# A fused attention and gated-MLP kernel: first batch pipelined by pairs of heads, first weights in fp32 behind it, last tokens of two batches moved into block 1

## Chip, cores, metric

The kernel runs on one core of one Trainium2 chip. The metric is the device time of one execution in microseconds (us). Each execution also records the mean clock that TensorE was granted, as a share of full speed.

Engine names: PE is TensorE (PEld its weight loads), DVE is VectorE, ACT is ScalarE, POOL is GpSimd, which issues the casting loads (fp32 read, fp16 written), SP is the engine that issues the first loads and the stores. A "strip" is one of the 12 groups of 128 hidden columns of the MLP; a "block" is 512 tokens of one batch that go through the MLP together. "Last tokens" are tokens 512 to 575 of a batch, which don't fill a group of 128; two batches share one.

## The reference, cut

```python
# q, k, v: (8 batches, 8 heads, 576 tokens, 64)
kv  = einsum('bhsd,bhse->bhde', k, v)
out = einsum('bhsd,bhde->bhse', q, kv)
x   = out / sqrt(mean(out * out, -1) + 1e-6) * g_norm      # then (4608, 512)
g, val  = x @ w_gate, x @ w_val                            # (512, 1536) each
ffn_out = (gelu(g) * val) @ w_out                          # (1536, 512)
y = x + sigmoid(x @ w_res) * ffn_out
```

## The kernel before

Where the traces were read for it, an engine ran its instructions in the order in which the program writes them. The attention of batch b is computed in small pieces that are put into "slots" between the MLP's strips of block b-1. Slots 0 to 11 of a block are its strips, the later ones its output rows. Block 0 is special: its output is accumulated strip by strip, so its slots run to 27.

The opening worked on batch 0 in halves of four heads, and the weights came by casting loads (fp32 in HBM, fp16 in SBUF) issued by GpSimd:

```python
for half in range(2):                      # fp32 loads on SP's queue, cast on the engines
    load_first("q", q, half)
    load_first("k", k, half)
    load_first_last(0, half)               # last tokens of k, v
    load_first_last(1, half)
    load_first("v", v, half)
# ... cast, transposes, kv, o, norm of one half, then of the other ...
nc.gpsimd.tensor_copy(out=hold, in_=s0["kv2"][0:1, 0, 0:1])   # waits for kv of half 0
load_wg(0)                                 # casting loads, 256 columns
load_wv(0)
# ... load_wg(i), load_wv(i), i = 1, 2, 3
```

The attention of batch 1, last tokens of batches 0 and 1 among it, all lay in block 0:

```python
plan = {                                   # NF = 12; attn_plan_1
    NF + 3: [attn_begin(1), a_qT(1, 0), a_qT(1, 1), load_batch(2), a_kv(1, 0, NP), a_rem_qT(1)],
    NF + 4: [a_rem_o(1), o[0]],            # a_rem_*: last tokens of two batches
    NF + 5: [o[1]], NF + 6: [o[2]], NF + 7: [o[3]],
    NF + 8: [a_norm(1), t[0], t[1], t[2], t[3], t[4]],
    2 * NF + 1: [x[0], x[1]],              # x: PE transposes of t, copied out by ACT
    2 * NF + 2: [x[2], x[3]],
    2 * NF + 3: [x[4]],                    # 27: behind the last step of block 0's output
}
# a_norm: 12 small DVE operations (a Newton iteration for 1/sqrt)
# plan_attn, batch 2 in block 1:
at(1, 2, by_token(2, "q"))                 # DVE: cast and reorder
at(1, 3, by_token(2, "k"), attn_begin(2), d_qT(2))
at(1, 4, a_kv(2, 0, 2))                    # PE: needs the cast k
# loads behind strip 2 of block 0, casting queue:
#   w_res, load_batch(1) = q, k, v, last tokens of k, v and of q (load_qr), then w_out in 3 pieces
```

## Time and profile before

| | before |
|---|---|
| median of 4 executions | 356.85 us (355.98 to 357.12) |
| span of the profiled execution | 354.6 us |
| busy share PE / DVE / ACT / POOL | 97% / 60% / 35% / 13% |
| third strip of block 0 starts | 23.35 us |
| first product with w_out | 47.07 us, after a wait of 0.60 |
| block 1's first product | 60.21 us |
| batch 2's kv product in block 1 | 69.14 us |
| first product of the last output row group | 347.60 us |

PE has work nearly all the time. The prediction below shows the page's lines.

### The profile page before, as it was taken

What the parts mean: (1) busy time and instruction counts of PE and PEld (TensorE: products, weight loads), DVE (VectorE), ACT (ScalarE), POOL (GpSimd) and SP (SyncE); (2) the same over time, 40 slices, a digit from 0 to 9 for tenths busy, and PEclk for the clock granted to TensorE, in tenths of its full rate; (3) what the DMA queues carried; (4) which work ended last, traced back from release to release, by engine and by line L of the source; (5) the groups of instructions that cost most, each with busy time, mean ns of one, the idle gap of its engine ahead of it and who ended that gap; (6) DMA issues with size and microseconds to landing.
All of it is one profiled execution on the core that took longest, in us unless ns stands there. A gap on an engine that the chain in (4) does not pass through costs nothing.

```text
span 354.6 us, 5021 instructions
## 1 busy us (share of the span) xinstructions
PE 343.0 (97%) x1905; PEld 168.9 (48%) x1905; DVE 214.1 (60%) x428; ACT 125.7 (35%) x215; POOL 47.7 (13%) x74
## 2 busy tenths in 40 slices
PE   6879999999999999999999999999999999999995
PEld 2554465454454445544554445444544444444443
DVE  5655448868757774676569656865587543343433
ACT  3653474253146222531363125422542233223320
POOL 1853330050050005000130023000000000000000
PEclk9999999999999999999999999999999999999999
DMA  8999999489699058904594369327000500020013
GB/s 250 221 180 201 193 203 142 137 137 106 160 164 131 2 133 167 153 0 118 136 166 36 86 169 175 24 61 194 0 2 30 133 31 0 30 87 5 1 31 89
DMA packets 77707, 37.95 MB, mean 107 GB/s; under 512 B 42226, under 2 KB 73202, under 8 KB 77682
## 3 DMA queue, kind: packets, MB, share of 16 engines
q0 software_dynamic: 39792, 17.70, 39.7%
q1 hardware_dynamic: 37728, 19.80, 20.6%
q8 instruction: 15, 0.25, 0.3%
q10 hardware_dynamic: 162, 0.13, 0.1%
q14 instruction: 10, 0.08, 0.1%
HBM read 38.80 MB, written 9.44 MB: 136 GB/s over the span
## 4 chain that ended last, share of the span: by engine, by line
PE 84%; DMA 9%; POOL 2%; DVE 1%; SPq 1%; ACT 0%; issue 0%; DVEq 0%
PE fps L348 25%; PE gps L315 23%; PE vps L315 23%; PE rps L335 8%; DMA wv<-in_moe_w_val_dram 4%; DMA wo<-in_moe_w_out_dram 4%; PE op L194 2%; PE kvp L165 2%; DMA vf<-in_v_dram 1%; POOL wg L120 1%; PE fps L377 1%; POOL wv L120 1%; PE orp L212 1%; PE kvp L172 0%; SPq L435 0%; DVE hid L304 0%
## 5 line engine op out<-in xcount | busy, mean ns | idle before, releaser
L315 PE MATMUL gps<-xT,wg 128*128 128x512 f16 (+2 forms) x448 | 112.3, 371 | 2.3 <-ACT xT L597 1.2
L304 DVE TENSOR_TENSOR hid<-ge,vps 128x512 f16<-128x512 f16 x108 | 73.5, 685 | 65.8 <-PE vps L315 59.3
L315 PE MATMUL vps<-xT,wv 128*128 128x512 f16 (+2 forms) x448 | 112.3, 371 | 0.0
L303 ACT ACTIVATE ge<-gps 128x512 f16<-128x512 f32 x108 | 64.4, 598 | 114.3 <-PE gps L315 105.2
L348 PE MATMUL fps<-wo,hid 128*128 128x512 f16 x420 | 96.9, 379 | 0.6 <-DMA wo<-in_moe_w_out_dram 0.6
L315 PEld LDWEIGHTS <-wv 128*128 128x128 f16 x448 | 43.4, 98 | 50.4 <-DMA wv<-in_moe_w_val_dram 0.3
L348 PEld LDWEIGHTS <-hid 128*128 128x128 f16 x420 | 40.8, 98 | 48.7 <-DMA wo<-in_moe_w_out_dram 0.8
L315 PEld LDWEIGHTS <-wg 128*128 128x128 f16 x448 | 42.0, 98 | 44.0 <-issue 2.7
L354 DVE SCALAR_TENSOR_TENSOR pf<-th,fps 128x512 f32<-128x512 f32 x35 | 23.8, 686 | 47.6 <-PE fps L348 47.6
L344 ACT ACTIVATE th<-rps 128x512 f32<-128x512 f32 x36 | 21.5, 598 | 79.5 <-PE rps L335 79.5
L335 PE MATMUL rps<-wr,xT 128*128 128x512 f16 x144 | 36.5, 379 | 0.0
L188 DVE TENSOR_REDUCE ss<-sq 128x8 f32<-128x512 f32 x32 | 21.5, 683 | 7.3 <-ACT sq L187 5.5
L359 DVE SCALAR_TENSOR_TENSOR osb<-pf,t 128x512 f32<-128x512 f32 x35 | 24.2, 691 | 1.1
L335 PEld LDWEIGHTS <-xT 128*128 128x128 f16 x144 | 14.1, 98 | 17.0
L187 ACT ACTIVATE sq<-op 128x512 f32<-128x512 f32 x28 | 16.7, 598 | 9.9 <-PE op L194 9.2
L727 POOL COPY hold<-qT 1x1 f16<-1x1 f16 x5 | 0.9, 177 | 138.2 <-DMA qT<-q 138.2
L252 DVE TENSOR_TENSOR t<-op,ny 128x512 f16<-128x512 f32 x28 | 17.8, 680 | 0.1
L271 DVE TENSOR_TENSOR t<-t,g 128x512 f16<-128x512 f16 x36 | 13.3, 417 | 0.0
L165 PE MATMUL kvp<-v,k 128*128 128x128 f16 x128 | 10.6, 219 | 2.4 <-DVE v L495 2.2
L165 PEld LDWEIGHTS <-k 128*128 128x128 f16 x128 | 8.9, 98 | 6.3 <-DVE v L495 1.9
L194 PEld LDWEIGHTS <-qT 128*128 128x128 f16 x112 | 8.4, 98 | 5.7
L194 PE MATMUL op<-kv,qT 128*128 128x128 f16 x112 | 10.8, 219 | 0.0
(96 smaller groups left out, 168.0 us busy)
## 6 DMA issues: line engine op xcount, KB each, us to landing
out_dram<-osb SPq DMA_DIRECT2D x32, 256.0 KB, 2.4
qraw<-in_q_dram POOLq DMA_DIRECT2D x7, 512.0 KB, 6.1
kraw<-in_k_dram POOLq DMA_DIRECT2D x7, 512.0 KB, 8.3
v<-in_v_dram POOLq DMA_DIRECT2D x7, 512.0 KB, 10.1
wo<-in_moe_w_out_dram POOLq DMA_DIRECT2D x3, 512.0 KB, 14.0
qf<-in_q_dram SPq DMA_DIRECT2D x2, 512.0 KB, 4.7
kf<-in_k_dram SPq DMA_DIRECT2D x2, 512.0 KB, 5.8
vf<-in_v_dram SPq DMA_DIRECT2D x2, 512.0 KB, 6.0
```

The source lines that it names most:

```text
L165: nc.tensor.matmul(ps, lhsT=k16[:, j, cs], rhs=v16[:, 2 * pr : 2 * pr + 2, j * D : (j + 1) * D], start=(j == 0), stop=False,)
L188: nc.vector.tensor_reduce(out=st[b]["ss"][:, j, :], in_=sq, op=ALU.add, axis=mybir.AxisListType.X)
L194: nc.tensor.matmul(ps[:, pr * P : (pr + 1) * P], lhsT=s["qT"][:, j, pr, :], rhs=s["kv2"][:, pr, :], start=True, stop=True)
L252: nc.vector.tensor_tensor(out=t_t[blk][:, jj, :].rearrange("p (h d) -> p h d", h=H), in0=s["o"][j].rearrange("p (h d) -> p h d", h=H), in1 ...
L303: nc.scalar.activation(out=ge, in_=gps, func=AF.Gelu)
L304: nc.vector.tensor_tensor(out=hids[blk][:, f, :], in0=ge, in1=vps, op=ALU.mult)
L315: nc.tensor.matmul(ps[:, j0 * P : j1 * P], lhsT=w[:, cc, :], rhs=xT_t[blk][:, j0:j1, cc, :], start=(cc == 0 and j0 == 0), stop=(cc == NP - ...
L335: nc.tensor.matmul(rps, lhsT=xT_t[blk][:, j, cc, :], rhs=wr16[:, cc, :], start=(cc == 0), stop=(cc == NP - 1),)
L344: nc.scalar.activation(out=th, in_=rps, func=AF.Tanh, scale=0.5)
L348: nc.tensor.matmul(fps, lhsT=hids[blk][:, f, j * P : (j + 1) * P], rhs=wo16[:, f, :], start=(f == 0), stop=(f == NF - 1))
L354: nc.vector.scalar_tensor_tensor(out=pf, in0=th, scalar=1.0, in1=fps, op0=ALU.add, op1=ALU.mult)
L359: nc.vector.scalar_tensor_tensor(out=osb, in0=pf, scalar=0.5, in1=t_t[blk][:, j, :], op0=ALU.mult, op1=ALU.add)
```

## The change

The intent: start on batch 0 sooner by loading and processing it in four pairs of heads; let the first weights follow on the same hardware queue, since SP is free to issue them early (in the kernel before its last load of the opening is issued by 7.22 us, and it issues no other before 40 us), and cast them on GpSimd and ACT; and take the last tokens of batches 0 and 1 out of block 0, with their loads behind w_out, so that w_out arrives sooner.

```diff
-for half in range(2): load_first("q", q, half) ... load_first("v", v, half)
+for i in range(2):
+    load_first_last(i, 0, nc.scalar)
+for pr in range(NP):                                   # 4 pairs
+    if pr == 2:
+        for i in range(2):
+            load_first_last(i, 1, nc.sync)
+    for which, t in (("q", q), ("k", k), ("v", v)):
+        load_first(which, t, pr)
+w_raw = {}                                             # first 256 columns, fp32
+for n, t in (("g", moe_w_gate), ("v", moe_w_val)):
+    ...
+    nc.sync.dma_start(out=w_raw[n], in_=t[:, 0 : WCS[0]].rearrange("(cc p) f -> p cc f", p=P))
...
+opening = """                                          # word: step, pair, [half], engine
+lc0P qc0A kc0A qT0 vc0D warm2 kv0 qc1P qo0D kvo0 warm1 kc1A o0 qT1 sq0 vc1D kv1 lc1P ...
+warm2 vc3D kv3 qo3A rd2 wcg0P kvo3 xT1 rt2 o3 xo1A ri2 t2 g0 wcg1P sq3a g1 wcv0P rd3a sq3b rd3b xT2 wcv1A
+w2 rt3 v0 xo2D gelu ri3 v1 t3a xT3a t3b v2 xo3aA xT3b xo3bD g2 w3 g3a v3a g3b v3b"""
...
 # attn_plan_1
-    NF + 3: [..., a_kv(1, 0, NP), a_rem_qT(1)],
-    NF + 4: [a_rem_o(1), o[0]], ...
-    NF + 8: [a_norm(1), t[0], t[1], t[2], t[3], t[4]],
+    NF + 3: [..., a_kv(1, 0, NP)],
+    NF + 4: [o[0], o[1]], ...
+    NF + 7: [a_norm(1, 0, NJ), t[0], t[1], t[2], t[3]],
     2 * NF + 1: [x[0], x[1]],
-    2 * NF + 2: [x[2], x[3]],
-    2 * NF + 3: [x[4]],
+    2 * NF + 3: [x[2], x[3]],
+at(1, 0, a_rem_qT(1))
+at(1, 1, a_rem_o(1))
+at(1, 2, a_norm(1, NJ, NJ + 1), t[NJ])                 # behind by_token(2, "q") in that slot
+at(1, 6, x[NJ])
+at(1, 7, a_x(1, NJ))
...
 for f in range(0, NF, 4):
     load_wo(f, f + 4)
+load_qr(0)                                             # no longer in the opening and load_batch(1)
+load_qr(1)
```

More of the change, by code (lines that the diff above doesn't have):

```diff
@@ L102, in load_batch @@
         load_last_kv(b)
-        load_qr(b)
+        if b > 1:
+            load_qr(b)
     def by_token(b, which):
@@ L222, in a_rem_o, with a_norm @@
         st[b]["o"][NJ] = o32
-    def a_norm(b):
+    def a_norm(b, j0, j1):
         s = st[b]
-        n = (NJ + (b % 2)) * H
-        ss = s["ss"].rearrange("p j h -> p (j h)")[:, 0:n]
+        if "rinv" not in s:
+            s["rinv"] = attnp.tile([P, NJ + 1, H], FP32, tag="ny", name="ny")
+        ss, yy = (t[:, j0:j1, :].rearrange("p j h -> p (j h)") for t in (s["ss"], s["rinv"]))
+        n = (j1 - j0) * H
         m = attnp.tile([P, (NJ + 1) * H], FP32, tag="nm", name="nm")[:, 0:n]
-        y = attnp.tile([P, (NJ + 1) * H], FP32, tag="ny", name="ny")
         a = attnp.tile([P, (NJ + 1) * H], FP32, tag="na", name="na")[:, 0:n]
         mh = attnp.tile([P, (NJ + 1) * H], FP32, tag="nh", name="nh")[:, 0:n]
-        yy = y[:, 0:n]
         nc.vector.tensor_scalar(out=m, in0=ss, scalar1=1.0 / D, scalar2=RMS_EPS, op0=ALU.mult, op1=ALU.add)
@@ L242, in a_norm @@
             nc.vector.scalar_tensor_tensor(out=yy, in0=a, scalar=1.5, in1=yy, op0=ALU.add, op1=ALU.mult)
-        s["rinv"] = y.rearrange("p (j h) -> p j h", h=H)
     def where(b, j):
@@ L425, with load_first, load_first_last @@
         raw[0, which] = t[:, 0 : H * NJ * D].rearrange("p (h x) -> p h x", h=H)
-    def load_first(which, t, half):
-        hs = slice(half * HH, (half + 1) * HH)
+    def load_first(which, t, pr):
+        hs = slice(2 * pr, 2 * pr + 2)
         nc.sync.dma_start(out=raw[0, which][:, hs, :], in_=rows4(t, 0, hs.start, hs.stop))
     last_raw = [consts.tile([R, H, D], FP32, name=f"{n}lf") for n in "kv"]
-    def load_first_last(i, half):
+    def load_first_last(i, half, queue):
         hs = slice(half * HH, (half + 1) * HH)
-        nc.sync.dma_start(
+        queue.dma_start(
             out=last_raw[i][:, hs, :], in_=(k, v)[i][0, hs, M0:S, :].rearrange("h s d -> s h d")
@@ L440 @@
     nc.scalar.dma_start(out=grow, in_=g_norm.unsqueeze(0))
-    for half in range(2):
-        load_first("q", q, half)
-        load_first("k", k, half)
-        load_first_last(0, half)
-        load_first_last(1, half)
-        load_first("v", v, half)
+    for i in range(2):
[8 more added lines that the diff above has]
+    for n, t in (("g", moe_w_gate), ("v", moe_w_val)):
+        r = "q" if n == "g" else "k"
+        w_raw[n] = stage.tile([P, H, NJ * D], FP16, tag=r + "raw", name=f"w{n}f")
+        w_raw[n] = w_raw[n].rearrange("p a b -> p (a b)").bitcast(FP32).rearrange("p (c f) -> p c f", c=NP)
+        nc.sync.dma_start(out=w_raw[n], in_=t[:, 0 : WCS[0]].rearrange("(cc p) f -> p cc f", p=P))
     ident32 = consts.tile([P, P], FP32, name="ident32")
@@ L489, with of_pair, f_cast @@
     first = {}
-    def f_cast(which, lo, hi, copy):
-        hs = slice(lo, hi)
+    tiles = {}
+    engines = {"A": nc.scalar.copy, "D": nc.vector.tensor_copy, "P": nc.gpsimd.tensor_copy}
+    def of_pair(pr):
+        return slice(2 * pr, 2 * pr + 2), slice(pr * P, (pr + 1) * P)
+    def f_cast(which, pr, copy):
+        hs, _ = of_pair(pr)
         dst, src = b16_t[0, which], raw[0, which]
@@ L500, in f_cast, with f_cast_last, f_qT @@
             )
-    def f_cast_last(half):
+    def f_cast_last(half, copy):
         hs = slice(half * HH, (half + 1) * HH)
         for i in range(2):
-            nc.gpsimd.tensor_copy(out=last_kv[0][i][0:R, hs, :], in_=last_raw[i][:, hs, :])
-    def f_qT(half):
+            copy(out=last_kv[0][i][0:R, hs, :], in_=last_raw[i][:, hs, :])
+    def f_qT(pr):
         q16 = b16_t[0, "q"].rearrange("p j h d -> p j (h d)")
-        for e2 in range(2):
-            pr = 2 * half + e2
-            first["qT", pr] = ps = pattn.tile([P, NJ, P], FP16, tag="at", name="qtp")
-            for j in range(NJ):
-                nc.tensor.transpose(ps[:, j, :], q16[:, j, pr * P : (pr + 1) * P], ident)
+        first["qT", pr] = ps = pattn.tile([P, NJ, P], FP16, tag="at", name="qtp")
+        for j in range(NJ):
+            nc.tensor.transpose(ps[:, j, :], q16[:, j, of_pair(pr)[1]], ident)
@@ L515, in f_qT_out, with f_kv, f_kv_out @@
     def f_qT_out(pr, copy):
         copy(out=s0["qT"][:, :, pr, :], in_=first["qT", pr])
-    def f_kv(half):
-        first["kv", half] = ps = pattn.tile([P, 2, P], FP32, tag="at", name="kvp")
-        for e2 in range(2):
-            kv_steps(0, ps[:, e2, :], 2 * half + e2)
-    def f_kv_out(half):
+    def f_kv(pr):
+        first["kv", pr] = ps = pattn.tile([P, P], FP32, tag="at", name="kvp")
+        kv_steps(0, ps, pr)
+    def f_kv_out(pr):
+        nc.vector.tensor_tensor(out=s0["kv2"][:, pr, :], in0=first["kv", pr], in1=mask, op=ALU.mult)
@@ new lines, in f_o, with f_sq @@
+    def f_o(pr):
+        pool, tag = (pmoe, "mm") if pr < 2 else (pattn, "at")
+        first["o", pr] = ps = pool.tile([P, NJ, P], FP32, tag=tag, name="op")
+        for j in range(NJ):
+            nc.tensor.matmul(
+                ps[:, j, :], lhsT=s0["qT"][:, j, pr, :], rhs=s0["kv2"][:, pr, :], start=True, stop=True
+            )
+    def f_sq(pr, j0, j1):
+        first["sq", pr, j0] = sq = attnp.tile([P, j1 - j0, 2, D], FP32, tag=f"sq{j1 - j0}", name="sq")
+        ps = first["o", pr].rearrange("p j (h d) -> p j h d", h=2)
+        nc.scalar.activation(out=sq, in_=ps[:, j0:j1], func=AF.Square)
@@ new lines, in f_red, with f_sqrt, f_rinv, f_t @@
+    def f_red(pr, j0, j1):
+        nc.vector.tensor_reduce(
+            out=s0["ss"][:, j0:j1, of_pair(pr)[0]], in_=first["sq", pr, j0], op=ALU.add, axis=mybir.AxisListType.X
+        )
+    def f_sqrt(pr):
+        at = (slice(None), slice(0, NJ), of_pair(pr)[0])
+        nc.scalar.activation(out=rms0[at], in_=s0["ss"][at], func=AF.Sqrt, bias=eps_col, scale=1.0 / D)
+    def f_rinv(pr):
+        hs, _ = of_pair(pr)
+        nc.vector.reciprocal(out=rinv0[:, :, hs], in_=rms0[:, :, hs])
+    def f_t(pr, j0, j1):
+        hs, cs = of_pair(pr)
@@ L524, in f_kv_out @@
         nc.vector.tensor_tensor(
-            out=s0["kv2"][:, 2 * half : 2 * half + 2, :],
-            in0=first["kv", half],
-            in1=mask[:, None, :].to_broadcast([P, 2, P]),
+            out=t0[:, j0:j1, cs].rearrange("p j (h d) -> p j h d", h=2),
+            in0=first["o", pr][:, j0:j1, :].rearrange("p j (h d) -> p j h d", h=2),
+            in1=rinv0[:, j0:j1, hs, None].to_broadcast([P, j1 - j0, 2, D]),
             op=ALU.mult,
         )
-    def f_o(half, j0, n, pool, tag):
-        first["o", half, j0] = ps = pool.tile([P, n, HH * D], FP32, tag=tag, name="op")
-        for j in range(n):
-            for e2 in range(2):
-                pr = 2 * half + e2
-                nc.tensor.matmul(
-                    ps[:, j, e2 * P : (e2 + 1) * P],
-                    lhsT=s0["qT"][:, j0 + j, pr, :],
-                    rhs=s0["kv2"][:, pr, :],
-                    start=True,
-                    stop=True,
-                )
@@ L545, in f_sq @@
-    def f_sq(half, j0, n):
-        first["sq", half, j0] = sq = attnp.tile([P, n, HH, D], FP32, tag=f"sq{n}", name="sq")
-        ps = first["o", half, j0]
-        nc.scalar.activation(out=sq, in_=ps.rearrange("p j (h d) -> p j h d", h=HH), func=AF.Square)
-    def f_red(half, j0, n):
-        nc.vector.tensor_reduce(
-            out=s0["ss"][:, j0 : j0 + n, half * HH : (half + 1) * HH],
-            in_=first["sq", half, j0],
-            op=ALU.add,
-            axis=mybir.AxisListType.X,
-        )
@@ L558, in f_sqrt @@
-    def f_sqrt(half, j0, n):
-        at = (slice(None), slice(j0, j0 + n), slice(half * HH, (half + 1) * HH))
-        nc.scalar.activation(out=rms0[at], in_=s0["ss"][at], func=AF.Sqrt, bias=eps_col, scale=1.0 / D)
-    def f_rinv(half, j0, n):
-        hs = slice(half * HH, (half + 1) * HH)
-        nc.vector.reciprocal(out=rinv0[:, j0 : j0 + n, hs], in_=rms0[:, j0 : j0 + n, hs])
-    def f_t(half, j0, n):
-        hs = slice(half * HH, (half + 1) * HH)
-        ps = first["o", half, j0]
-        for j in range(n):
-            nc.vector.tensor_tensor(
-                out=t0[:, j0 + j, half * HH * D : (half + 1) * HH * D].rearrange("p (h d) -> p h d", h=HH),
-                in0=ps[:, j, :].rearrange("p (h d) -> p h d", h=HH),
-                in1=rinv0[:, j0 + j, hs, None].to_broadcast([P, HH, D]),
-                op=ALU.mult,
-            )
@@ L577, in f_xT_tile @@
-    def f_xT_tile(half, j0, n, pool, tag):
-        first["xT", half, j0] = pool.tile([P, 2, n, P], FP16, tag=tag, name="xtp")
-    def f_xT_pe(half, j0, n):
-        ps = first["xT", half, j0]
-        for j in range(n):
-            for e2 in range(2):
-                cc = 2 * half + e2
-                nc.tensor.transpose(ps[:, e2, j, :], t0[:, j0 + j, cc * P : (cc + 1) * P], ident)
-    def f_xT(half, j0, n, pool, tag):
-        f_xT_tile(half, j0, n, pool, tag)
-        f_xT_pe(half, j0, n)
@@ L591, in f_xT_out, with f_xT @@
-    def f_xT_out(half, j0, n, on_vector):
-        ps = first["xT", half, j0]
-        dst = xT0[:, j0 : j0 + n, 2 * half : 2 * half + 2, :].rearrange("p j c t -> p c j t")
-        if on_vector:
+    def f_xT(pr, j0, j1):
+        first["xT", pr, j0] = ps = pattn.tile([P, j1 - j0, P], FP16, tag="at", name="xtp")
+        for j in range(j0, j1):
+            nc.tensor.transpose(ps[:, j - j0, :], t0[:, j, of_pair(pr)[1]], ident)
+    def f_xT_out(pr, j0, j1, eng):
+        dst, ps = xT0[:, j0:j1, pr, :], first["xT", pr, j0]
+        if eng == "D":
@@ L597, in f_xT_out, with f_mm, f_piece @@
             nc.scalar.activation(out=dst, in_=ps, func=AF.Copy, scale=gcol)
-    keep_warm(7)
+    def f_mm(ws, i, pr, j0, j1):
+        for f in range(2):
+            if (f, i) not in tiles:
+                tiles[f, i] = [pmoe.tile([P, NJ * P], FP32, tag="mm", name="gv"[i] + "ps"), 0]
+            ps, done = tiles[f, i]
+            tiles[f, i][1] = done = done + j1 - j0
+            nc.tensor.matmul(
+                ps[:, j0 * P : j1 * P],
+                lhsT=w_of(ws, f)[:, pr, :],
+                rhs=xT0[:, j0:j1, pr, :],
+                start=(done == j1 - j0),
+                stop=(done == NP * NJ),
+            )
+    def f_piece(word):
+        name = word.rstrip("0123abADP")
+        rest = word[len(name) :]
+        pr = int(rest[0])
+        j0, j1 = {"a": (0, NJ // 2), "b": (NJ // 2, NJ)}.get(rest[1:2], (0, NJ))
+        eng = rest[-1]
+        if name in ("qc", "kc", "vc"):
+            f_cast(name[0], pr, engines[eng])
+        elif name == "lc":
+            f_cast_last(pr, engines[eng])
+        elif name == "warm":
+            keep_warm(int(rest))
+        elif name == "w":
+            load_wg(pr)
+            load_wv(pr)
+        elif name in ("wcg", "wcv"):
+            cs = slice(2 * pr, 2 * pr + 2)
+            engines[eng](out=(wg_c if name == "wcg" else wv_c)[0][:, cs, :], in_=w_raw[name[-1]][:, cs, :])
+        elif name == "qo":
+            f_qT_out(pr, engines[eng])
+        elif name in ("qT", "kv", "kvo", "o", "rt", "ri"):
+            {"qT": f_qT, "kv": f_kv, "kvo": f_kv_out, "o": f_o, "rt": f_sqrt, "ri": f_rinv}[name](pr)
+        elif name in ("sq", "rd", "t", "xT"):
+            {"sq": f_sq, "rd": f_red, "t": f_t, "xT": f_xT}[name](pr, j0, j1)
+        elif name == "xo":
+            f_xT_out(pr, j0, j1, eng)
+        elif name == "g":
+            f_mm(wg_c, 0, pr, j0, j1)
+        elif name == "v":
+            f_mm(wv_c, 1, pr, j0, j1)
+    keep_warm(5)
     gcol = consts.tile([P, 1], FP32, name="gcol")
@@ L607 @@
     nc.tensor.matmul(gps, lhsT=ones16, rhs=grow16.rearrange("p h d -> p (h d)"), start=True, stop=True)
-    f_cast("q", 0, HH, nc.scalar.copy)
-    f_qT(0)
-    f_cast("k", 0, HH, nc.vector.tensor_copy)
-    f_qT_out(0, nc.scalar.copy)
-    f_qT_out(1, nc.scalar.copy)
-    nc.vector.tensor_copy(out=g16, in_=gps)
-    f_cast_last(0)
-    f_cast("v", 0, HH, nc.vector.tensor_copy)
-    keep_warm(7)
-    f_kv(0)
-    f_kv_out(0)
-    f_cast("q", HH, H, nc.scalar.copy)
-    keep_warm(2)
-    f_o(0, 0, 2, pmoe, "mm")
@@ L622 @@
-    f_o(0, 2, 2, pmoe, "mm")
-    hold = consts.tile([1, 1], FP16, name="hold")
-    nc.gpsimd.tensor_copy(out=hold, in_=s0["kv2"][0:1, 0, 0:1])
-    load_wg(0)
-    load_wv(0)
-    f_cast("k", HH, H, nc.gpsimd.tensor_copy)
-    f_cast_last(1)
-    for i in range(1, len(WCS)):
-        load_wg(i)
-        load_wv(i)
-    f_sq(0, 0, 2)
-    f_sq(0, 2, 2)
-    f_red(0, 0, 2)
-    f_red(0, 2, 2)
-    f_sqrt(0, 0, 2)
-    f_sqrt(0, 2, 2)
-    f_qT(1)
-    f_qT_out(2, nc.scalar.copy)
-    f_qT_out(3, nc.scalar.copy)
@@ L642 @@
-    f_cast("v", HH, H, nc.vector.tensor_copy)
-    f_rinv(0, 0, 2)
-    f_t(0, 0, 2)
-    keep_warm(9)
-    f_kv(1)
-    f_kv_out(1)
-    keep_warm(1)
-    f_xT(0, 0, 2, pmoe, "mm")
-    f_xT_out(0, 0, 2, False)
-    f_rinv(0, 2, 2)
-    f_t(0, 2, 2)
-    f_o(1, 0, 2, pattn, "at")
-    f_o(1, 2, 2, pattn, "at")
-    f_sq(1, 0, 2)
-    f_sq(1, 2, 2)
-    f_xT_tile(0, 2, 2, pattn, "at")
-    f_red(1, 0, 2)
-    f_red(1, 2, 2)
-    f_sqrt(1, 0, 2)
-    f_rinv(1, 0, 2)
-    f_t(1, 0, 2)
+    nc.vector.tensor_copy(out=g16, in_=gps)
@@ L664, in first_gval @@
+    keep_warm(3)
+    opening = """
+    lc0P qc0A kc0A qT0 vc0D warm2 kv0 qc1P qo0D kvo0 warm1 kc1A o0 qT1 sq0 vc1D kv1 lc1P qo1A rd0 kvo1 qc2P
+    warm2 rt0 o1 kc2P qT2 ri0 sq1 t0 vc2A rd1 xT0 qc3P kv2 qo2A xo0D kvo2 rt1 kc3P qT3 o2 ri1 sq2 t1 w1
+    warm2 vc3D kv3 qo3A rd2 wcg0P kvo3 xT1 rt2 o3 xo1A ri2 t2 g0 wcg1P sq3a g1 wcv0P rd3a sq3b rd3b xT2 wcv1A
+    w2 rt3 v0 xo2D gelu ri3 v1 t3a xT3a t3b v2 xo3aA xT3b xo3bD g2 w3 g3a v3a g3b v3b
+    """
     def first_gval():
         hids[0] = hidp.tile([P, NF, NJ * P], FP16, tag="hid", name="hid")
-        tiles = [pmoe.tile([P, NJ * P], FP32, tag="mm", name=n) for n in ("gps", "vps", "gps", "vps")]
@@ L670, in part @@
-        def part(j0, j1, c0, c1):
-            for f in range(2):
-                m_mm(tiles[2 * f], wg_c, f, 0, j0, j1, c0, c1)
-                m_mm(tiles[2 * f + 1], wv_c, f, 0, j0, j1, c0, c1)
-        part(0, 2, 0, 2)
-        f_xT_pe(0, 2, 2)
-        f_xT_out(0, 2, 2, False)
-        f_sqrt(1, 2, 2)
-        f_rinv(1, 2, 2)
-        f_t(1, 2, 2)
-        part(2, NJ, 0, 2)
-        for j in range(NJ):
-            f_xT(1, j, 1, pattn, "at")
-            f_xT_out(1, j, 1, j % 2 == 1)
-            if j == 2:
+        for word in opening.split():
+            if word == "gelu":
@@ L686, in first_gval @@
                 nc.scalar.preload_act_table_set("gelu_and_others")
-            if j > 0:
-                part(j - 1, j, 2, NP)
-        part(NJ - 1, NJ, 2, NP)
+            else:
+                f_piece(word)
         for f in range(2):
-            m_act(0, f, tiles[2 * f], tiles[2 * f + 1])
-        load_qr(0)
+            m_act(0, f, tiles[f, 0][0], tiles[f, 1][0])
     def attn_plan_1():
@@ L709, in attn_plan_1 @@
                 lambda: a_kv(b, 0, NP),
-                lambda: a_rem_qT(b),
             ],
-            NF + 4: [lambda: a_rem_o(b), o[0]],
-            NF + 5: [o[1]],
-            NF + 6: [o[2]],
-            NF + 7: [o[3]],
-            NF + 8: [lambda: a_norm(b), t[0], t[1], t[2], t[3], t[4]],
+            NF + 4: [o[0], o[1]],
+            NF + 5: [o[2]],
+            NF + 6: [o[3]],
+            NF + 7: [lambda: a_norm(b, 0, NJ), t[0], t[1], t[2], t[3]],
             2 * NF + 1: [x[0], x[1]],
-            2 * NF + 2: [x[2], x[3]],
-            2 * NF + 3: [x[4]],
-        }
-        return plan, [lambda j=j: a_x(b, j) for j in range(NJ + 1)]
+            2 * NF + 3: [x[2], x[3]],
+        }
+        at(1, 0, lambda: a_rem_qT(b))
+        at(1, 1, lambda: a_rem_o(b))
+        at(1, 2, lambda: a_norm(b, NJ, NJ + 1), t[NJ])
+        at(1, 6, x[NJ])
+        at(1, 7, lambda: a_x(b, NJ))
+        return plan, [lambda j=j: a_x(b, j) for j in range(NJ)]
     plans = [{} for _ in range(B + 1)]
+    hold = consts.tile([1, 1], FP16, name="hold")
     def load_behind(b):
@@ L759, in plan_attn @@
             at(m, o0 + j, lambda j=j: a_o(b, j))
-        at(m, n0, lambda: a_norm(b))
+        at(m, n0, lambda: a_norm(b, 0, NJ + b % 2))
         n0 += 1 if b == 2 else 2
```

## The prediction

> **What bounds the kernel now.** I read the page first (busy shares, the 40 slices, the chain), then what PE waits for, then the timeline and the stretches of the first 75 us, where the change works.
>
> ```profile
> PE 343.0 (97%) x1905; PEld 168.9 (48%) x1905; DVE 214.1 (60%) x428; ACT 125.7 (35%) x215; POOL 47.7 (13%) x74
> PE   6879999999999999999999999999999999999995
> ```
>
> The reader is to see that PE is full from the fourth slice to the last but one. No other engine is near it. So a microsecond is won or lost only where PE has nothing to do, which is in the opening and at a few waits. The waits of PE over the whole run are few (columns: who waited for what, total us, times, longest):
>
> ```profile
> PE kvp L165 <- DVE v L495: 2.2, 2, 1.4
> PE gps L315 <- ACT xT L597: 1.2, 2, 0.8
> PE gps L315 <- ACT ge L303: 0.9, 1, 0.9
> PE fps L348 <- DMA wo<-in_moe_w_out_dram: 0.6, 1, 0.6
> ```
>
> The first three lie in the opening, the last at 47 us. The opening ends where the third strip of hidden columns begins its product with the gate weights, at 23.35 us in the timeline:
>
> ```profile
> 23.35 1.02 PE L315 MATMUL gps<-xT,wg 128*128 128x512 f16 x4 [0.85 <-ACT ge L303]
> ```
>
> From there on PE runs gap-free but for 0.6 us at 47 us and a few tenths elsewhere. The work of PE after this point is the same in both kernels (small transposes and products of the last tokens only move within it), so the change in time is: the shift of this point, plus the change in later waits.
>
> The DMA is the second bound, in the first 47 us only. Stretches (us; busy us of PE, PEld, DVE, ACT, POOL; granted clock; DMA share; GB/s as written):
>
> ```profile
> 2.50:13.00 10.50, 8.21 (x60) 4.21 (x58) 5.68 (x16) 4.83 (x9) 3.42 (x6) 1.00 1.12 326
> 13.50:17.00 3.50, 2.62 (x29) 1.92 (x29) 3.00 (x9) 1.98 (x4) 3.50 (x6) 1.00 1.11 135
> 17.00:21.00 4.00, 2.77 (x37) 2.40 (x35) 2.98 (x9) 1.88 (x6) 4.00 (x6) 1.00 1.20 156
> 25.00:30.00 5.00, 5.00 (x25) 2.24 (x23) 2.06 (x3) 1.61 (x4) 1.51 (x3) 1.00 1.24 206
> ```
>
> [...]The fp32 loads of batch 0 move 326 GB/s, the casting loads of wide weight rows 206, those of the narrow first two weight pieces (256 columns) only 135 to 156. GpSimd's waits show landings in order: third value piece at 27.43 us (needed by PE at 27.66), first third of w_out at 47.02 (PE waited 0.60 for it). So the opening cannot be shortened by more than the transfers also gain.
>
> [...]the twelve operations of a norm on only 32 columns take 2.34 us (82.40 to 84.74 us).
>
> **The change part by part.**
>
> *Opening by pairs, weights behind on the hardware queue.* A pair's tensor is 0.26 MB, so pair 0 can start about 0.7 us sooner and PE's wait for v shrinks. The last pair lands when all 3.41 MB are in, near 13.4 us as before (v's second half was cast at 13.46). Its chain, from durations scaled from the timeline: cast 0.4, kv products 0.5, mask 0.3, o 0.4, squares and sums in two halves 1.6, sqrt and reciprocal 0.5, t 0.4, transposes 0.3, copy 0.4; about 18.2 us. The weights: 1.05 MB in fp32 behind it at 326 to 380 GB/s is 2.8 to 3.2 us, so the value half lands near 17, or 17.6 because the second weight piece, issued by GpSimd near 13.3, takes a share. A cast of half a tensor on GpSimd is about 0.55 us (1.07 for twice that): 18.2 again. Then 12 matmuls of 512 and 8 of 256 columns, 2.6 and 0.9 us, some of them done earlier: the opening ends near 21.1, and the next strip, which waits for the first gelu, starts at 21.6. That is 1.75 us sooner than 23.35.
>
> *Does the DMA allow it?* Between 12.9 and 24.0 us the before kernel moved the first two narrow pieces and one wide one; a wide one is 2.55 us (24.89 to 27.43), so the narrow ones took some 4.2 us each against 3.0 for the fp32 load: the stream is ahead by an estimated 1.2 us. The third value piece then lands at 26.2 instead of 27.43, and PE, which needs it 4.31 us after the strip of 23.35, cannot effectively be more than 1.5 us ahead. I take **1.5 us**.
>
> *Loads of the last tokens behind w_out.* Each costs about 0.4 us of the stream (32.48 to 35.47 us holds one of them and a 1 MB piece of 2.55). Two fewer ahead of w_out, with 1.2 from above: landing at 45.0. PE, without the four transposes of the last tokens, is ready at 46.25 - 1.5 = 44.75. The wait of 0.60 becomes about 0.2: **0.4 us** won.
>
> *Boundary of block 0 and block 1.* In the kernel before, transposes of rows 2 and 3 stand before the last step of w_out, and only those of the last tokens after it. In the changed order all four products of the last step come first, then eight transposes, then at once block 1's first product, which reads all four rows. The same pair in the trace costs:
>
> ```profile
> 57.05 0.72 PE L264 MATMUL xtp<-ident,t 128*128 128x128 f16 x8
> 57.48 1.26 ACT L265 ACTIVATE xT<-xtp,gcol 128x512 f16<-128x512 f16 x2 [4.81 <-PE xtp L264]
> ```
>
> From 57.05 to 58.74 is 1.69 us, of which 0.44 is PE's own work. PE idles 1.3 us where it idled 0.2: **1.1 us lost**.
>
> *Last tokens in block 1.* Their norm (twelve small operations, some 2.1 us at 8 columns) and their t (0.6) now stand on DVE in strip 2 of block 1, ahead of the cast of batch 2's k, which PE's kv product needs two strips later. Before:
>
> ```profile
> 68.40 0.69 DVE L106 COPY k<-kraw 128x2048 f16<-128x2048 f16 x1
> ...
> 69.14 0.40 PE L165 MATMUL kvp<-v,k 128*128 128x128 f16 x4
> ```
>
> There PE already waited some 0.3 us for this cast; the order on the engines shows the same place for both. From block 1's first product (60.21) the cast ended 8.88 us later. Added: 0.66 for PE's moved products ahead of it, 0.5 for DVE waiting on the squares of the last tokens, 2.7 for norm and t: 12.75. PE is at that product after 8.63 + 0.66 = 9.3. It waits about 3.5 us instead of 0.3, and DVE catches up during the wait: **3.2 us lost**.
>
> Sum: -1.5 - 0.4 + 1.1 + 3.2 = +2.4; 356.74 + 2.4 = 359.1.
>
> **Rivals.** (1) The opening decides. If DVE's order in block 1 does no harm, because the casts and norm overlap more closely than I add up, the time is 356.7 - 1.9 + 1.1 = about 356. For it: DVE is only 60% busy. Against it: [...]the cast stands behind the norm. (2) The transfers swallow the opening's gain: [...]the third weight piece is issued only after GpSimd's casts, later than before (near 18 against 15.82), and lands no sooner. Then the gain is 0.4 at most and the time 360.5. (3) A cold TensorE: [...]in the first 4 us of the trace a 512-column one takes 0.43 us instead of 0.22. If the opening's products run at that pace, it ends up to 2 us later; 360 to 361. (4) The opening is far better than I think (20 us, transfers in time): 357.5, unless the losses are also smaller.
>
> **Range and chances.** 359.0 us. Losses of 3.3 to 5, gains of 0.5 to 3.5: from 355.6 to 361.4, eight times in ten. 2% is 7.1 us, which is more than the whole opening's idle time can give, and the losses need to double for it: faster 0.03, within 2% 0.93, slower 0.04.
>
> **What would show it.** Right: PE waits on the cast of k by DVE some 3 us in block 1 (longest wait of PE in the run), over 1 us on ACT's copy of xT at the block boundary; the third strip starts between 21 and 22.5; w_out lands near 45 us. Wrong: no such wait in block 1, or an opening that ends before 20 or after 23.

The pace behind "12 matmuls of 512 and 8 of 256 columns" is the trace's: groups of four matmuls of 512 columns start 0.86 us after one another (61.07, 61.94 and 62.80 us in the kernel before).

## The result

| | before | changed |
|---|---|---|
| median | 356.85 us | 360.83 us (359.37 to 361.62, 4 executions) |
| ratio | | 1.0111, interval 1.0071 to 1.0151 |
| span of the profiled execution | 354.6 us | 357.6 us |

Ratios here and below are the mean time of one kernel's executions over that of the other's in the same rounds, so not quite the ratio of the medians. Executions over 1.5% slower than the fastest of the same kernel are left out of the means. The changed kernel is slower by 1.1%, which is within 2%.

The page of the changed kernel looks like the one before; PE's row has a short dip in the seventh and in the eighth slice and stays full after:

```profile
PE 342.8 (96%) x1866; PEld 167.0 (47%) x1866; DVE 216.3 (60%) x442; ACT 124.7 (35%) x216; POOL 49.3 (14%) x78
PE   8699998699999999999999999999999999999995
```

What PE waited for says where (us in total, times, longest):

```profile
PE kvp L166 <- DVE k L107: 3.5, 1, 3.5
PE idle L488 <- DVE zeros L459: 1.2, 1, 1.2
PE gps L315 <- ACT xT L265: 1.1, 1, 1.1
PE kvp L166 <- ACT qT L528: 1.1, 1, 1.1
...
PE fps L348 <- ACT qT L157: 0.5, 1, 0.5
```

The first and the third of these are the two places that the prediction named. PE's timeline has them:

```profile
22.05 1.02 PE L315 MATMUL gps<-xT,wg 128*128 128x512 f16 x4 [0.36 <-ACT ge L303]
...
45.54 1.04 PE L348 MATMUL fps<-wo,hid 128*128 128x512 f16 x4 [0.48 <-ACT qT L157]
...
58.99 1.02 PE L315 MATMUL gps<-xT,wg 128*128 128x512 f16 x4 [1.13 <-ACT xT L265]
...
71.93 0.40 PE L166 MATMUL kvp<-v,k 128*128 128x128 f16 x4 [3.48 <-DVE k L107]
```

The third strip starts 1.30 us sooner (22.05 against 23.35). The wait in front of w_out is 0.48; the profile names ACT there, but the weight load that PE needs first also waited on w_out's transfer (0.6 us in the list of waits), and several other runs name the transfer at this place (0.4 to 0.6 us in experiments 1, 2 and 5 to 8). At the block boundary and at batch 2's kv product stand the new waits. On DVE the cast of k has moved behind the norm and t of the last tokens:

```profile
66.22 0.69 DVE L107 COPY q<-qraw 128x2048 f16<-128x2048 f16 x1
66.82 0.17 DVE L235 TENSOR_SCALAR nm<-ss 128x8 f32<-128x8 f32 x1
...
68.84 0.17 DVE L243 SCALAR_TENSOR_TENSOR ny<-na,ny 128x8 f32<-128x8 f32 x1
69.04 0.69 DVE L252 TENSOR_TENSOR t<-o,ny 128x512 f16<-128x512 f32 x1
69.65 0.68 DVE L359 SCALAR_TENSOR_TENSOR osb<-pf,t 128x512 f32<-128x512 f32 x1
70.25 0.42 DVE L271 TENSOR_TENSOR t<-t,g 128x512 f16<-128x512 f16 x1
70.59 0.68 DVE L304 TENSOR_TENSOR hid<-ge,vps 128x512 f16<-128x512 f16 x1
71.19 0.69 DVE L107 COPY k<-kraw 128x2048 f16<-128x2048 f16 x1
```

From 66.82 to 69.04 is the norm, 2.22 us for twelve operations on eight columns. They take 0.17 us each and start 0.20 after one another, but for two; on 32 columns, four times the work, the prediction read 2.34 us for the same twelve. The cast of k ends at 71.88 and PE goes on at 71.93.

The accounts of the profiled execution, in PE idle time: opening -1.30; from there to w_out's first product 23.49 us against 23.72, of which 0.22 are four transposes that moved away, so 0.0; from there to block 1's first product 13.45 against 13.14 us although 0.66 of work moved away, so +0.97; from there to the kv product 12.94 against 8.93 with 0.66 of work moved in, so +3.35. The last 0.22 of moved work follows behind the kv product (278.68 us from there to the last output row group, against 278.46). Together +3.0 in idle time, and with all the moved work cancelling, this is the difference of the spans. The medians differ by 4.0 us. The last microsecond is not in these waits.

### The profile page after: what moved, and what is told of

It reads as the page before. It is cut to its first block, busy times and chain, and to the rows that moved or that the text cites. A ratio compares the mean times of both kernels' runs of the same rounds, so it can differ in the third digit from the quotient of the medians.

```text
span 357.6 us, 4967 instructions
## 1 busy us (share of the span) xinstructions
PE 342.8 (96%) x1866; PEld 167.0 (47%) x1866; DVE 216.3 (60%) x442; ACT 124.7 (35%) x216; POOL 49.3 (14%) x78
## 4 chain that ended last, share of the span: by engine, by line
PE 90%; DMA 3%; DVE 2%; ACT 2%; POOL 1%; issue 1%; SPq 1%; DVEq 0%
PE fps L348 25%; PE gps L315 25%; PE vps L315 25%; PE rps L335 9%; DMA kf<-in_k_dram 3%; PE op L195 2%; PE kvp L166 2%; PE fps L377 1%; SPq L429 1%; ACT qT L157 1%; PE gps L592 1%; PE orp L213 1%; PE kvp L173 0%; DVE hid L304 0%; ACT xT L265 0%
## 5 line engine op out<-in xcount | busy, mean ns | idle before, releaser
L315 PE MATMUL gps<-xT,wg 128*128 128x512 f16 x424 | 108.8, 379 | 1.5 <-ACT xT L265 1.1
L315 PE MATMUL vps<-xT,wv 128*128 128x512 f16 x424 | 108.8, 379 | 0.0
L315 PEld LDWEIGHTS <-wv 128*128 128x128 f16 x424 | 41.4, 98 | 50.2 <-DMA wv<-in_moe_w_val_dram 0.4
L315 PEld LDWEIGHTS <-wg 128*128 128x128 f16 x424 | 39.9, 98 | 42.4 <-issue 1.8
## 6 DMA issues: line engine op xcount, KB each, us to landing
v<-in_v_dram POOLq DMA_DIRECT2D x7, 512.0 KB, 10.2
```

What stands on the lines that cost most here:

```text
L315: nc.tensor.matmul(ps[:, j0 * P : j1 * P], lhsT=w[:, cc, :], rhs=xT_t[blk][:, j0:j1, cc, :], start=(cc == 0 and j0 == 0), stop=(cc == NP - ...
```

## The experiments

All kernels gave correct results. In what follows "the two mends" are the edits of the first and second experiment.

### 1. Norm of the last tokens later

```diff
-at(1, 2, a_norm(1, NJ, NJ + 1), t[NJ]); at(1, 6, x[NJ]); at(1, 7, a_x(1, NJ))
+at(1, NF + 1, a_norm(1, NJ, NJ + 1), t[NJ]); at(2, 4, x[NJ]); at(2, 5, a_x(1, NJ))
```

> The changed kernel, with the norm and t of the last tokens moved from strip 2 of block 1 to behind its second output row. My theory: the 3.5 us wait of PE for the cast of k goes back to under 0.5, the time falls by 3.2 us against the changed kernel, and lands within 1 us of the kernel before (ratio 0.998 to 1.003). Rival (the changed kernel's slowness is a lower granted clock in most of its runs, or lies later in the run): the wait goes but the time stays over 359 us.

Measured: median 356.70 us, ratio 1.001 (0.9998 to 1.0022). PE's wait for k is 0.66 us. Against the changed kernel's ratio of 1.0111 that is 3.6 us won, a little more than the 2.8 us of shorter wait. The rival, a loss later in the run or in the clock alone, is out for the larger part. Its clocks are low all the same, 0.990 to 0.999: in its profile (0.990) the granted clock was 0.66 from 10 to 20 us, in the opening, and 1.00 after 20 us. It cost little there: the third strip started at 22.27, and an execution at 0.999 took 356.69 us against 356.82. So a low mean clock alone does not say where the slow stretch was, nor that it cost time.

### 2. Transposes of block 1's rows earlier

```diff
-2 * NF + 3: [x[2], x[3]],
+2 * NF + 2: [x[2], x[3]],
```

> The changed kernel, with the transposes of block 1's rows 2 and 3 back ahead of the last step of w_out. Theory: the 1.1 us wait of PE for ACT's copy at the block boundary shrinks to about 0.2, nothing else moves, 0.9 us less than the changed kernel (ratio to the kernel before about 1.006 to 1.009). Rival: DVE's release of the accumulators binds the same place anyway, and less than 0.4 us is won.

Measured: the wait at the boundary is 0.27 us, as expected, but the median is 360.22 us and the ratio 1.0116 (1.0098 to 1.0135): nothing won. The profile shows why, and it is not the rival. These are PE's lines around the wait for k:

```profile
66.35 1.03 PE L315 MATMUL vps<-xT,wv 128*128 128x512 f16 x4
70.85 0.61 PE L166 MATMUL kvp<-v,k 128*128 128x128 f16 x4 [3.48 <-DVE k L107]
...
71.89 1.91 PE L315 MATMUL gps<-xT,wg 128*128 128x512 f16 x4
73.60 1.91 PE L315 MATMUL vps<-xT,wv 128*128 128x512 f16 x4
...
76.37 0.82 PE L315 MATMUL gps<-xT,wg 128*128 128x512 f16 x3
```

Four matmuls take 1.91 us behind the wait instead of 1.03, and the next group starts 1.71 later instead of 0.86. In the stretches of this profile (us; busy us of five engines; granted clock; DMA share; GB/s) the clock is half:

```profile
66.50:70.90 4.40, 0.93 (x6) 0.25 (x4) 4.13 (x14) 0.60 (x1) 0.00 (x0) 0.85 0.18 58
70.90:75.90 5.00, 5.00 (x24) 2.79 (x25) 2.04 (x5) 0.60 (x1) 1.70 (x3) 0.50 0.61 159
75.90:85.00 9.10, 9.10 (x62) 5.03 (x60) 6.43 (x11) 5.06 (x9) 3.20 (x5) 0.97 1.37 176
```

Half the clock over 5 us is 2.5 us of PE work lost. The distance from the kv product to the first product of the last output row group shows the same: 352.21 - 70.85 = 281.36 us, 2.68 more than the changed kernel's 350.61 - 71.93 = 278.68. The profiled execution of the changed kernel had the same wait and no such stretch (clock 1.00 from 71.90 to 75.90), but its other executions had mean clocks of 0.994, 0.986 and 0.991. So the new theory is that the wait costs twice: once as idle time and, in many executions, again as a slow restart.

### 3. Both mends

> Both edits of the two runs above in the changed kernel. Theory: the two losses are independent and add, 4.1 us less than the changed kernel in the profile: a span near 353.5, ratio to the kernel before 0.996 to 0.998, the best of all so far. Rival (losses overlap, or DVE or PE finds a new wait in block 1 or 2): the sum of the gains is under 3 us and it doesn't beat the kernel before.

Measured: median 355.78 us, ratio 0.9983 (0.9971 to 0.9995), clocks 0.998 to 1.0 in all five. It beats the kernel before by a little less than expected. In its profile both waits have shrunk together, to 0.66 and 0.27 us, so the two losses are independent. PE still waits 0.66 us for k, against 0.13 in the kernel before (69.14 less 69.01, the end of the product ahead of it), which the expectation had left out.

### 4. The new opening alone

The changed kernel with `attn_plan_1`, the loads of the last tokens and their place as in the kernel before; only the opening is new.

> Only the new opening (pairs, fp32 weights on the hardware queue) in the kernel before: last tokens, their loads and the transposes as they were. Theory: third strip starts at 22.05 as in the changed kernel, but w_out comes with the loads of the last tokens ahead of it, so it lands about 0.8 us later than in the changed kernel (near 46.3) and the wait there grows from 0.5 to about 1.1 us. Net against the kernel before: -1.3 + 0.5 = -0.8 us, ratio 0.997 to 0.999. Rival (the opening is the loss, the deferral harmless): slower than the kernel before by 1 us or more.

Measured: median 356.31 us, ratio 1.0007 (0.9978 to 1.0036): the opening alone gains nothing on average. Its times spread from 355.24 to 358.10, and the profile is of an execution of 356.85. It does start the third strip sooner (21.91), but w_out is no sooner here:

```profile
44.87 0.39 PE L204 MATMUL qtrp<-ident,qr 128*128 128x128 f16 x4
47.57 1.04 PE L347 MATMUL fps<-wo,hid 128*128 128x512 f16 x4 [2.31 <-DMA wo<-in_moe_w_out_dram]
```

It is 0.5 us later than before (47.57 against 47.07), with everything behind the first weights as in the kernel before, and 2.0 later than in the changed kernel (45.54). So two numbers of the prediction are wrong, as far as one profile shows. The new opening's lead in the stream of transfers doesn't reach w_out: the third value piece landed at 26.68, 0.75 sooner than the 27.43 of the kernel before, but w_out's first product is later. And the two loads of last tokens ahead of w_out cost it 2.0 us, not 0.8. Experiment 10 tests the second again.

### 5. The cast of k ahead of the norm

```diff
-at(1, 2, by_token(2, "q"))            # then norm and t of the last tokens
-at(1, 3, by_token(2, "k"), ...)
+at(1, 2, by_token(2, "q"), by_token(2, "k"))
```

> The changed kernel, with the cast of k put ahead of the norm of the last tokens in strip 2 of block 1; the norm stays there. Theory (DVE in strip 2 has more to do than the buffered accumulators allow): PE's wait for the cast goes, but the products of strip 3 are multiplied on DVE 0.6 us later than now, so PE waits about 2.1 us for the release of an accumulator in strip 5; [...]the granted clock stays at 0.998 or more in all runs. About 2 us less than the changed kernel's median: ratio to the kernel before 1.004 to 1.007. Rival (only the order of cast and norm matters): no wait over 0.7 us in block 1, ratio 0.999 to 1.002.

Measured: median 359.85 us, ratio 1.0104 (1.0074 to 1.0133): no better than the changed kernel. The wait for k is gone, and PE stands 2.27 us two strips later, at the product of q and kv:

```profile
74.93 0.44 PE L195 MATMUL op<-kv,qT 128*128 128x128 f16 x4 [2.27 <-DVE t L271]
75.17 0.63 PE L264 MATMUL xtp<-ident,t 128*128 128x128 f16 x4
75.59 1.91 PE L315 MATMUL gps<-xT,wg 128*128 128x512 f16 x4
```

The size is as expected, the place is not (I had named an accumulator in strip 5): DVE is behind, and the mask product of kv comes late (in this trace it ends at 74.58, and the t that the profile names, the operation after it, at 74.91). So the order of cast and norm is not the matter; the norm doesn't fit into this strip. My expectation for the clock, which rested on no run here, failed: four matmuls take 1.91 us here too, and from 74.90 to 78.70 the granted clock is 0.55. A wait of 2.27 us was enough here. Over its six executions, time does not go with the mean clock: 360.89 us came at 0.998 and 357.77 at 0.997. What set these apart stays open.

### 6. The wait filled with idle matmuls

```diff
+ps = pattn.tile([P, C], FP32, tag="at", name="fill")
+for _ in range(14):                   # useless work, ahead of a_kv(2, 0, 2) in block 1
+    nc.tensor.matmul(ps, lhsT=zeros[:, 0:P], rhs=zeros, start=True, stop=True)
```

> The changed kernel with 14 idle 512-column matmuls (3.0 us at full clock) on PE ahead of the product that waits for the cast of k. They do no useful work and only fill the wait. Theory (the clock halves after the 3.5 us without work in some executions, as the second experiment's profile shows with four matmuls in 1.91 us behind the wait): the wait remains as idle work, so no gain from the wait itself, but the granted clock is 0.997 or more in all runs, the spread of the times shrinks to 0.7 us or less, and the median falls to 359.2 to 359.7, some 1 us under the changed kernel. Rival (the spread and lower clock come from the opening or from elsewhere): clocks of 0.985 to 0.995 in half of the runs as before, median over 360.

Measured: median 359.10 us (358.81 to 360.00), ratio 1.0079 (1.0066 to 1.0093); clocks 0.998 to 1.0 in all five executions.

```profile
68.89 3.18 PE L732 MATMUL fill<-zeros 128*128 128x512 f16 x14
72.53 0.40 PE L166 MATMUL kvp<-v,k 128*128 128x128 f16 x4 [0.46 <-DVE k L107]
...
73.10 1.03 PE L315 MATMUL gps<-xT,wg 128*128 128x512 f16 x4
```

PE reaches the kv product no sooner, and the products behind it run at full speed. The median was forecast at 359.2 to 359.7; the spread is 1.2 us rather than 0.7. From the kv product to the last output row group it takes 351.21 - 72.53 = 278.68 us, as in the changed kernel's profile without a slow stretch. Here the useless work on the waiting engine kept the clock and took nothing away from the rest. Experiment 12 repeats the unaltered kernel, in later rounds and on another chip.

### 7. Both mends, cast of k one strip earlier

Experiments 3 and 5 together: with the norm gone from strip 2, the earlier cast has room.

> Both mending edits (norm late, transposes early) and the cast of k one strip earlier, directly behind that of q. With the norm gone from this strip there is room on DVE: the remaining wait of 0.66 us for k goes to 0, no new one comes. Span 353.4, ratio to the kernel before 0.994 to 0.997. Rival: hid of strip 3 comes 0.6 us later and PE waits for it, no gain over the two edits alone.

Measured: median 354.11 us (353.78 to 355.39), ratio 0.9946 (0.9931 to 0.9962). The wait for k is gone and no other has come in block 1. The profile's span is 352.4 us, a microsecond under the forecast; half of that is its third strip, which started at 21.55. This start varies between 21.3 and 22.3 over the profiles that have this opening with the loads behind w_out, so a single profile's start is good to about half a microsecond. It is the best version, 0.54% under the kernel before.

### 8. Last tokens of batch 0 by casting loads

In the kernel of experiment 7, two casting loads by GpSimd at the start take the place of four fp32 loads and four casts.

> As the run before, and the last tokens of batch 0's k and v come by two casting loads on the otherwise idle GpSimd queue at the start, instead of four fp32 loads on the other two queues and four casts. Theory (the small-row loads delay the pairs' loads and hold the issuing queue for 1.4 us each two): v of pair 3 lands about 1 us sooner, third strip starts at 21.0 to 21.5 instead of 22.05; but w_out then bounds again, so only 0.3 to 0.6 us of it reaches the end. Rival (the casting queue's small rows are as slow, and compete just so): start at 22.0 or later, no gain.

Measured: median 355.44 us, ratio 0.998 (0.9962 to 0.9999), worse than experiment 7 by 0.34%. The rival is right:

```profile
10.20 0.22 PE L173 MATMUL kvp<-vl,kl 128*128 128x128 f16 x1 [2.53 <-DMA vl<-in_v_dram]
```

The last tokens of v arrive at 10.2 us; in the changed kernel they were cast by 8.2. The third strip starts at 23.67 in the profiled execution, the slowest of the six (357.00 us), with a mean clock of 0.987: behind the wait of 2.53 us groups of four products of 128 columns start 0.37 us before the next at 12.79 us, against 0.22 at 10.80, and two idle matmuls of 512 columns take 1.06 us at 16.02; at 19.74 four take 1.03. So this start holds a slow stretch too. This path was a miss.

### 9. First weights on the casting queue

In the kernel of experiment 7, `load_wg(0)` and `load_wv(0)` are issued by GpSimd near 9 us, and the fp32 loads and casts of the first weights are gone.

> The best version so far (both mends, cast of k early), with the first weights not in fp32 behind batch 0 on the hardware queue but through the casting queue as in the kernel before, issued when GpSimd is free near 9 us; pairs stay. Theory of the prediction (narrow weight rows are slow on the casting queue[...]): the opening gets later, third strip at 22.5 to 23.5, and w_out about 1 us later; the time rises by 0.7 to 1.5 us. Rival (the fp32 route gains nothing in the stream, only the pairs matter): third strip at 22 or sooner, w_out as before or sooner, no slower.

Measured: median 356.33 us, ratio 1.0007 (0.9985 to 1.003), 2.2 us slower than experiment 7 by the ratios. The direction is as predicted and the size is larger. The weights now move beside the pairs and hold up the last one: PE waits for the cast of its v.

```profile
18.11 0.59 PE L166 MATMUL kvp<-v,k 128*128 128x128 f16 x4 [2.67 <-DVE v L509]
...
25.31 1.02 PE L315 MATMUL gps<-xT,wg 128*128 128x512 f16 x4 [0.36 <-ACT ge L303]
```

Behind this wait four matmuls of 512 columns took 1.88 us at 19.56, against 1.03 at 21.50, and the mean clock of this execution was 0.990, so 25.31 is wait and slow clock together; one profile doesn't part them. That the hardware queue helps by its order, pairs first and weights behind, fits the wait for v, and is argued from it.

### 10. Loads of the last tokens ahead of w_out

In the kernel of experiment 7, `load_qr(0)` stands behind the opening and `load_qr(1)` in batch 1's loads, as in the kernel before. Their use stays in block 1.

> The best version so far, with the two loads of the last tokens' q back ahead of w_out (one behind the opening, one in batch 1's loads); their use stays in block 1. Nothing else moves. By the prediction each costs 0.4 us of the stream: w_out's wait grows from 0.43 to 1.3 us. By the fourth experiment (wait 2.3 us, landing 47.5) they cost 1.0 each: the wait grows to about 2.4 us, time up by 1.9 us.

Measured: median 357.39 us, ratio 0.9999 (0.9971 to 1.0027): 1.9 us slower than experiment 7 by the ratios, as experiment 4 had it. The spread is wide (355.11 to 357.88). In the profiled execution the third strip started at 22.97 and PE waited 1.37 us for w_out, and 1.0 for a weight piece ahead of it. From the third strip to w_out's first product it took 48.39 - 22.97 = 25.42 us against 44.93 - 21.55 = 23.38 in experiment 7: 2.0 us for two loads of 64 KB as written. The distance was 23.4 to 24.0 in all eight profiles of this opening with the loads behind w_out, and 25.66, 0.22 of it moved work, in experiment 4, so it is not chance. But two of the six executions took only 355.1 us; these were not profiled, and what they paid for the loads is open.

### 11. The old opening with the mended deferral

The kernel before, with loads behind w_out, norm late, cast of k early and transposes early.

> The kernel before with its old opening, and the deferral of the last tokens in the mended form (loads behind w_out, norm late, cast of k early, transposes early). Theory (opening and deferral need each other): third strip at 23.35 as before; w_out lands at 45.0 to 45.5, before PE needs it at 46.2, so its 0.6 us wait goes; with the 0.3 us wait for k gone too: 0.9 us less than the kernel before, ratio 0.997 to 0.998. The best version should then be 1.3 us faster still by its opening. Rival: the mended deferral alone brings the whole 2.1 us.

Measured: median 355.87 us, ratio 0.998 (0.9968 to 0.9992), 0.7 us under the kernel before; no wait for w_out is left in PE's list. The third strip started at 23.91 in its profile, not at 23.35 as expected, with the same opening. With experiments 4 and 7 this completes a square:

| | last tokens as before | deferral, mended |
|---|---|---|
| old opening | 1 (kernel before) | 0.9980 (experiment 11) |
| new opening | 1.0007 (experiment 4) | 0.9946 (experiment 7) |

Alone the opening gives nothing and the deferral 0.7 us; together they give 1.9. The opening needs the deferral, since w_out would otherwise take its gain back. Two cautions. The three kernels were measured in different rounds on three chips, each against the kernel before, and what the two edits give beyond the plain sum is 1.5 us, give or take 1.3 (an estimate from the three ratios and their intervals). And the right column also casts k one strip earlier, which was not tried on the kernel before alone.

### 12. The changed kernel again

> The changed kernel itself, unaltered, once more, for its clock and spread in the same rounds as the others. If the halved clock behind the 3.5 us wait is the rest of its loss: clocks between 0.985 and 1.0, times between 359.2 and 362, the slower ones those with the lower clock, median 360 to 361 against 359.1 with the filled wait. If not: time doesn't go with the clock.

Measured: median 360.72 us (358.77 to 362.27), ratio 1.0116 (1.009 to 1.0142). The ten executions of the changed kernel, by clock:

| mean granted clock | times, us |
|---|---|
| 0.999 | 358.77, 359.37 |
| 0.994 to 0.995 | 360.20, 360.24, 360.39, 361.04 |
| 0.986 to 0.991 | 361.42, 361.62, 361.81, 362.27 |

The groups don't overlap. The profiled execution is one of the middle group, and the slow stretch is behind the wait for k:

```profile
71.29 0.40 PE L166 MATMUL kvp<-v,k 128*128 128x128 f16 x4 [3.47 <-DVE k L107]
...
71.86 1.86 PE L315 MATMUL gps<-xT,wg 128*128 128x512 f16 x4
73.51 1.91 PE L315 MATMUL vps<-xT,wv 128*128 128x512 f16 x4
...
351.65 2.79 PE L377 MATMUL fps<-wo,hid 128*128 128x256 f16 x24
```

The first profile of the changed kernel, at clock 0.999, has after the same wait:

```profile
72.50 1.03 PE L315 MATMUL gps<-xT,wg 128*128 128x512 f16 x4
...
350.61 2.78 PE L377 MATMUL fps<-wo,hid 128*128 128x256 f16 x24
```

From the kv product to the last output row group it is 278.68 us in the first profile and 351.65 - 71.29 = 280.36 in this one: the slow restart cost 1.68 us. The middle group's mean is 1.4 us above the first group's. In experiment 2's profile, at 0.990, it cost 2.68, with a clock of 1.00 before the wait; the lowest group's mean is 2.7 above the first. So the restart alone is large enough for both groups, but the lowest was not profiled, and a slow stretch in the opening (experiment 1) can lower a mean clock too; there it stays open.

With the wait filled the same kernel had no clock under 0.998 and a median 1.6 us lower (359.10). By the ratios to the kernel before, each in its own rounds (1.0079 and 1.0116), it is 1.3. The fill is the only edit. Together with the two profiles this makes the slow restart the cause of most of the last microsecond.

## Why the prediction was right or wrong

The time of 360.83 us lies within the range, 1.8 above the forecast of 359.0, and the chance of "within 2%" was 0.93. The main mechanism, a norm on DVE ahead of the cast that PE waits for, was named with its place and its size before the run. By its steps:

| step | predicted | in the profile |
|---|---|---|
| third strip starts | 21.6 us, 1.5 of the gain taken | 22.05 us, 1.30 |
| wait for w_out and on the way there | 0.4 won, landing at 45.0 | 0.0 won, product at 45.54 |
| boundary of the blocks | 1.1 lost | 0.97 lost |
| wait for the cast of k | 3.5 us, 3.2 lost | 3.48 us, 3.35 lost |
| sum | +2.4 | +3.0 |
| slow restart after the wait | not in the sum | +1.0 in the medians, most of it (1.68 in one profile) |

- **The cast of k** was right in size and kind. Experiment 1 shows it by taking the norm away; experiment 5 shows that the norm's 2.2 us on DVE is the cause rather than the order of two lines.
- **The boundary** was right; experiment 2 shrinks the wait to 0.27 us, and experiments 1 and 3, which differ by just this edit, differ by 0.9 us in their medians.
- **The opening** was right within half a microsecond, in part by luck. The weights were cast by 18.16 us (18.2 forecast), but the last pair's v could be cast only at 15.00 (13.4 forecast), and its last copy ended at 20.78 instead of 18.2. This hardly showed, since by then only a few products were left. Rival 3, a slow TensorE in the opening, did not decide: matmuls ran at the slow pace until about 8.4 us (0.43 us for 512 columns, though the recorded clock there is 1.00), but the profile's chain of waits goes through the transfers of k until 14.14 us and then through GpSimd's casts and load issues until 17.11. Rival 2, that the third weight piece lands no sooner, was wrong (26.71 against 27.43); that w_out takes the opening's gain back is what experiment 4 shows without the deferral.
- **The step "loads of the last tokens behind w_out"** failed in both of its terms, and the errors hid each other. "Each costs about 0.4 us of the stream" measured 1.0 on average (experiments 4 and 10). "With 1.2 from above" for the stream being ahead measured 0.7 at the third value piece, and 0.5 late at w_out (experiment 4). Landing at 45.0 was forecast from a sum of two wrong parts, and 45.5 came: luck.
- **The sum was too small** by what no step had: the clock. The prediction put a slow TensorE only into the opening (rival 3) and nothing behind its own wait of 3.5 us. The restart came in one of two profiles of the changed kernel, behind a wait of 3.47 us (clock 0.58 for 4 us), and eight of its ten executions had a mean clock of 0.995 or less. That the clock would stay high behind a shorter wait, as I expected in experiment 5, was wrong there: behind 2.27 us it was 0.55 for 3.8 us. The length of the wait alone does not decide: 3.48 us in the first profile of the changed kernel, and 2.31 us in that of experiment 4, left the clock at 1.00. What exactly trips the clock stays open.

## What to carry to other kernels

When work is moved into a place where one engine is loaded and another waits, add up the receiving engine's queue between the two instructions that the waiting engine needs; small dependent operations counted here by their number rather than their size (twelve took 2.22 us on 8 columns and 2.34 us on 32). In two of three profiles a wait of 3.5 us on TensorE cost half to three quarters of its length again in the restart (1.68 and 2.68 us), and 14 idle matmuls in this wait won 1.3 us by the ratios, so compare the granted clock of every execution, not only the profiled one, and then look in a profile where it was low. An opening that starts sooner is worth only what the next transfer allows: in experiment 4 the third strip started 1.4 us sooner, w_out's first product came 0.5 us later, and nothing was gained. Here opening and deferral had to come together, and with two mends and an earlier cast they beat the kernel before by 1.9 us.
